# Attention and experts on one core: the last four blocks' attention in even steps, tiles merged before the exponent

## The chip, the cores and the metric

One core of a Trainium2 chip. The metric is the time of one execution on the device in microseconds (us); the kernel before takes 918.2 us, the median of 3 runs (917.75 to 921.53). TensorE (PE in the profile) multiplies matrices, VectorE (DVE), ScalarE (ACT) and GpSimd (POOL) work on elements, SyncE (SP) issues the DMAs.

## The reference

```python
# q, k, v: (4, 8, 576, 64); window of 128 keys, causal
scores = scale * q @ k.T
scores = where(mask, scores + slopes * -(distance), -1e9)      # mask: 0 <= rel < 128
attn = exp(scores - max(scores))
attn = attn / (sum(attn) + 1e-9)
x = (attn @ v)            # as (2304, 512): 4 x 576 tokens, 8 heads x 64
p = domain_probs / (sum(domain_probs) + 1e-9)                  # (2304, 4)
for e in range(4):        # w1: (4, 512, 1024), w2: (4, 1024, 512)
    out += p[:, e] * (relu(x @ w1[e]) @ w2[e])
```

All in float32. The kernel splits each float32 operand into a rounded high part and the remainder (names ending in h and l) and forms each product as three matmuls.

## The kernel before

The 2304 tokens are 18 tiles of 128, put together in seven blocks (`BLOCKS`): 0 to 2 of 256 tokens, 3 to 6 of 384. The attention of a block is done head pair by head pair (4 of them), tile by tile: a *unit* is one tile for two heads. The experts' weights come in 16 pieces of 256 hidden columns; `passes` sets in which order pieces meet blocks: first block 0 alone, then 0 and 1, then 0 to 2, then 1 and 2, then 2, then all pieces with blocks 3 and 4, then with 5 and 6. A meeting of a piece and a block is a *step*: `hidden` (matmuls at line 907, ReLU at 928 on ScalarE, remainder at 935 on VectorE) and `output` (matmuls at 1095, weighted sum into `acc` at 1113 on VectorE). From the ninth piece on, blocks 3 and 4 are multiplied together by a scheme of seven products (`sevenfold`, line 985), and blocks 5 and 6 from the second piece on; `differences` prepares it.

A planner (`Plan`) makes the order. Every operation has the engines that it can run on with an assumed duration, the data that it reads and writes, buffers out of fixed pools, and a due time. `order` simulates the engines and takes what can start earliest, and among those the one that is due first; instructions are then issued in that order, fixed for each engine. Operations that read two SBUF tiles on VectorE, and those of GpSimd, are kept apart by `port`. The due times run on a scale of expert matmuls alone: a step of 256 tokens counts 5.55, one of 384 tokens 8.33, and `opened[nb]` is where block nb's first step stands: 38.9, 94.4, 266.6 for blocks 1, 2, 3 (and 4), 524.9 for 5 (and 6). The attention of a block is due evenly over `spans[nb]`, less `MARGIN` = 10; `end` is the first sevenfold step, 399.9, less `AHEAD` = 30.

A unit outside block 0 goes: `scores` (line 513, two keys' tiles: the tile before and its own, 256 columns for each head), `least` for each head (544 on VectorE: bias added, sign turned, minimum kept), `exponents` (556 on ScalarE, with the sum), 1e-9 added to the two sums (571), reciprocal (580), weights (601 or 609), transposes (627), split in two parts and put in place with the mask (311, 323, 651 on GpSimd), and for the segment the products with v (698). In a row exactly one of a column's two keys, 128 apart, lies in the window; so from block 2 on (`fold`) the two halves of `s` are added after the exponent (592), and the rest works on 128 columns.

`gathered` sums the heads' parts (722, 725), casts the result to `xh` and takes the remainder `xl` (through `cast`, line 311 and 313, and `minus`, line 323). `xh` and `xl` have two places of 768 tokens: blocks 0 to 2 are group 0, 3 and 4 group 1, 5 and 6 group 2, which takes a place when its former group has been read for the last time.

Of the kernel before, what the change touches and what calls it, by code (L numbers as in the profile page):

```python
# [11 lines left out]
AF = mybir.ActivationFunctionType  # L12
ALU = mybir.AluOpType
# [3 lines left out]
NEG = -1.0e30  # L17
PE, DVE, ACT, POOL, SP = "PE", "DVE", "ACT", "POOL", "SP"
# [169 lines left out]
dve = lambda n: 0.065 + n / 960  # L188
dve2 = lambda n: 0.065 + n / 1920
pool = lambda n: 0.1 + n * 0.00256  # L190
# [4 lines left out]
BLOCKS = ((0, 256), (256, 256), (512, 256), (768, 384), (1152, 384), (1536, 384), (1920, 384))  # L195
# [7 lines left out]
FOLD = 2  # L203
# [25 lines left out]
def attention_moe(  # L229
# [13 lines left out]
    nc = tc.nc  # L243
    P = 128
# [4 lines left out]
    NPAIR = H // 2  # L249
# [7 lines left out]
    plan = Plan()  # L257
# [38 lines left out]
    bias = sb.tile([P, H, 2 * P], F32, tag="bias", name="bias")  # L296
# [9 lines left out]
    def cast(o, i, n, due, reads, writes, sbuf=True):  # L306


        def emit(e):
            if e == ACT:  # L310
                nc.scalar.activation(o(), i(), AF.Copy)  # L311
            else:
                nc.vector.tensor_copy(o(), i())

        plan.op(
            {ACT: act(n), DVE: dve2(n) if sbuf else dve(n)}, emit, due, reads, writes, port=(DVE,) if sbuf else ()
        )
# [55 lines left out]
    gs = []  # L373
# [6 lines left out]
    spans = {0: (-30.0, -6.0)}  # L380
    spans[1] = (5.0, opened[1])
    spans[2] = (opened[1], opened[2])
    spans[3] = (opened[2], (opened[2] + opened[3]) / 2)
    spans[4] = ((opened[2] + opened[3]) / 2, opened[3])
    end = opened[5]
    if SEVEN[3, 4] < NU:
        end = next(now for l, nb, now in steps if nb == (3, 4)) - AHEAD
    spans[5] = (opened[3], (opened[3] + end) / 2)
    spans[6] = ((opened[3] + end) / 2, end)
    for nb, (s0, n) in enumerate(BLOCKS):  # L390
        for hp in range(NPAIR):
            g = Rec()
# [94 lines left out]
    def unit(u):  # L487
# [36 lines left out]

        bkey = [("bias", g.hp)] if pk else [("bias", g.hp, 1)]
        bv = lambda: bias[:, hs, :]
        if edge:
# [7 lines left out]
            )  # L537
            bv, bkey = b2, [bb]
        if 0 < pk < P:
            plan.op({POOL: 0.3, DVE: 0.28}, lambda e: by[e].memset(sv()[:, :, :o], 0.0), d, ["scores"], both, port=())  # L540


        def least(h):
            return lambda e: nc.vector.tensor_tensor_reduce(  # L544
                out=sv()[:, h, o:],
                in0=sc()[:, h, :n],
                in1=bv()[:, h, o:],
                scale=-0.125,
                scalar=-NEG,
                op0=ALU.add,  # L550
                op1=ALU.min,
                accum_out=t[:, h : h + 1],
            )

        def exponents(h):
            return lambda e: nc.scalar.activation(  # L556
                sv()[:, h, o:],
                sv()[:, h, o:],
                AF.Exp,
                bias=t[:, h : h + 1],  # L560
                scale=-1.0,
                accum_out=t[:, 2 + h : 3 + h],
            )

        for h in range(2):
            plan.op({DVE: 0.15 + n / 960}, least(h), d + 0.3, [*bkey, bk], [(s, h), (t, h)])
        for h in range(2):
            plan.op({ACT: 0.29 + n * 0.00087}, exponents(h), d + 0.4, [(t, h)], [(s, h), (t, 2 + h)])
        plan.op(
            {DVE: 0.19},  # L570
            lambda e: nc.vector.tensor_scalar(  # L571
                out=t[:, 2:4], in0=t[:, 2:4], scalar1=1.0e-9, scalar2=None, op0=ALU.add
            ),
            d + 0.5,
            [],
            [(t, 2), (t, 3)],
# [5 lines left out]
            [(t, 2), (t, 3)],  # L582
            [(t, 4)],
        )


        fold = pk > 0 and g.nb >= FOLD
        o2, n2 = (P, P) if fold else (o, n)
        if fold:
            plan.op(  # L590
                {DVE: dve(2 * P), POOL: pool(2 * P)},
                lambda e: by[e].tensor_tensor(out=sv()[:, :, P:], in0=sv()[:, :, P:], in1=sv()[:, :, :P], op=ALU.add),  # L592
                d + 0.5,
                [(t, 2), (t, 3)],
                both,
                port=(DVE, POOL),
            )

        def weights_(e):
            if e == DVE:  # L600
# [133 lines left out]
    def gathered(g):  # L734

        n, d = g.n, g.units[-1].due
        gr, at = divmod(g.s0, GROUP)
        xh, xl = groups.setdefault(gr, (Buf("xh"), Buf("xl")))
        cols = slice(at, at + n)
        if g.plain:  # L740

            for h, r in ((0, lo64), (1, hi64)):
                part = (g.nb, g.hp, h)
                xparts.setdefault((g.nb, g.hp), []).append(part)
                cast(
                    lambda r=r: xh[r, g.hp, cols],
                    lambda h=h, r=r: g.av[h][r, :n],
                    n,
                    d + 1.6,
                    [(g.av, h)],  # L750
                    [(xh, part)],
                    False,
                )
                minus(
                    lambda r=r: xl[r, g.hp, cols],
                    lambda h=h, r=r: g.av[h][r, :n],
                    lambda r=r: xh[r, g.hp, cols],
                    n,
                    d + 1.7,
                    [(g.av, h), (xh, part)],  # L760
                    [(xl, part)],
                    False,
                )
            return
        x = Buf("x")
        xs = [(x, 0), (x, 1)]
        summed(g, n, d, lambda: x[:, :n], xs)
        part = (g.nb, g.hp)
        xparts.setdefault((g.nb, g.hp), []).append(part)
        cast(lambda: xh[:, g.hp, cols], lambda: x[:, :n], n, d + 1.6, xs, [(xh, part)])  # L770
        minus(
            lambda: xl[:, g.hp, cols],
            lambda: x[:, :n],
            lambda: xh[:, g.hp, cols],
            n,
            d + 1.7,
            [*xs, (xh, part)],
            [(xl, part)],
        )


# [79 lines left out]
    def differences(nbs, due):  # L861

        xh, xl = groups[BLOCKS[nbs[0]][0] // GROUP]
        done = seen_all() + [(t, p) for t in (xh, xl) for nb in nbs for hp in range(NPAIR) for p in xparts[nb, hp]]
        n = BLOCKS[nbs[0]][1]
        B = lambda t, d, b: f(t[:, 2 * d : 2 * d + 2, b * n : b * n + n])
        tv = lambda b: b[:, :, :n]
        add, sub = ALU.add, ALU.subtract
        raw = {}
        T = kept[nbs] = {}  # L870

        def steps_(name, first_, *rest):
            t = raw[name] = Buf("k")
            a, b, op, rd = first_
            plus(lambda: tv(t), a, b, 2 * n, due, [*done, *rd], [t], op)
            for b2, op2 in rest:
                plus(lambda: tv(t), lambda: tv(t), b2, 2 * n, due, [*done], [t], op2)
            hk, lk = Buf("th"), Buf("tl")
            hv, lv = (lambda: hk.place), (lambda: lk.place)
            cast(hv, lambda: tv(t), 2 * n, due, [t, *done], [hk])  # L880
            minus(lv, lambda: tv(t), hv, 2 * n, due, [t, hk, *done], [lk])
            T[name] = (hv, lv, hk, lk)

        steps_(1, (lambda: B(xh, 0, 1), lambda: B(xh, 0, 0), sub, []), (lambda: B(xl, 0, 1), add), (lambda: B(xl, 0, 0), sub))
        t1 = raw[1]
        steps_(2, (lambda: B(xh, 1, 1), lambda: tv(t1), sub, [t1]), (lambda: B(xl, 1, 1), add))
        t2 = raw[2]
        steps_(3, (lambda: B(xh, 1, 1), lambda: B(xh, 0, 1), sub, [T[2][2]]), (lambda: B(xl, 1, 1), add), (lambda: B(xl, 0, 1), sub))
        steps_(4, (lambda: B(xh, 1, 0), lambda: tv(t2), sub, [t2]), (lambda: B(xl, 1, 0), add))
# [308 lines left out]
        ["dp", "dps"],  # L1198
        ["prob"],
    )  # L1200
    for g in gs:
        segment(g)
        for u in g.units:
            unit(u)
        gathered(g)
    if joint:
        for nbs in dict.fromkeys(joint.values()):
            differences(nbs, first[min(l for l in joint if joint[l] == nbs)] - WEARLY)
    for l in range(len(loads)):
        weights(l)  # L1210
    outs = []
    for l, nb, due in [*steps, (None, None, now)]:
        half = (len(outs) + 1) // 2
        if l in joint:
            sevenfold(l, due, [[o for j, o in enumerate(outs) if (SLOT[j] if len(outs) > 3 else 2 * j + 1) == i] for i in range(7)])
        else:
            if l is not None:
                hidden(l, nb, 0, due)
            for o in outs[:half]:
                output(*o, due)  # L1220
            if l is not None:
                hidden(l, nb, 1, due + 2)
            for o in outs[half:]:
                output(*o, due + 2)
        if l is not None:
            outs = [(l, b, i) for b in (nb if l in joint else [nb]) for i in range(BLOCKS[b][1] // P)]
# [67 lines left out]
```

## Time and profile before

| what | us |
| --- | --- |
| median of 3 runs | 918.2 |
| the profiled execution | 917.55 |
| its span in the trace | 915.8 |
| TensorE busy | 890.8 (97%) |
| VectorE busy | 735.0 (80%) |
| ScalarE busy | 454.3 (50%) |
| GpSimd busy | 378.4 (41%) |

The span runs from the first to the last instruction of one execution. Busy times are unions of the recorded instructions; matmuls overlap in the record, and a short wait between two of them can lie under the end of the first. The granted clock of TensorE is 1.00 of full speed (the 2.4 GHz level) in all stretches shown here. Idle time has, where the trace shows it, the instruction that ended it behind an arrow.

### The profile page before, as it was taken

Reading aid. Unit: us, or ns where it says so; the run is one execution under the profiler, and the core shown is the slowest. Engines: PE = TensorE matmul, PEld = TensorE weight load, DVE = VectorE, ACT = ScalarE, POOL = GpSimd, SP = SyncE. Lnnn points to the kernel's source line nnn. Section 1 sums busy time; section 2 is a strip of 40 time slices with the busy share of each in tenths; the row PEclk is TensorE's granted clock in tenths of the full one; section 3 lists DMA queues with packets and bytes.
Section 4 is the critical chain, followed back from the end, with each engine's and each line's share of the span. In section 5 each row is a group of like instructions: output and inputs, shape, how many; then the busy total and the mean of one; then the engine's idle time right before and its main releaser. Section 6 shows DMA issues by size and latency. Waiting matters only on the chain.

```text
span 915.8 us, 14430 instructions
## 1 busy us (share of the span) xinstructions
PE 890.8 (97%) x5108; PEld 805.5 (88%) x5108; DVE 735.0 (80%) x1520; ACT 454.3 (50%) x1089; POOL 378.4 (41%) x361
## 2 busy tenths in 40 slices
PE   7898999999999999989999999999999999999998
PEld 5787999999999998878899998989898998999897
DVE  4999887697888899989997997767876767677665
ACT  4976555364655466656664343435333433434341
POOL 2446545244444355577674663212632222222100
PEclk9999999999999999999999999999999999999999
DMA  9764534242444445443211022221232121212101
GB/s 241 234 213 160 176 123 137 81 136 67 136 135 135 131 155 178 157 127 98 82 49 67 24 90 72 68 70 52 87 116 92 47 93 47 89 50 76 40 1 70
DMA packets 39961, 96.20 MB, mean 105 GB/s; under 512 B 3792, under 2 KB 17488, under 8 KB 39888
## 3 DMA queue, kind: packets, MB, share of 16 engines
q1 hardware_dynamic: 39888, 95.28, 32.6%
q8 instruction: 40, 0.66, 0.3%
q14 instruction: 33, 0.27, 0.1%
HBM read 90.54 MB, written 4.72 MB: 104 GB/s over the span
## 4 chain that ended last, share of the span: by engine, by line
PE 84%; DVE 12%; ACT 2%; issue 1%; DMA 1%; ACTq 0%; DVEq 0%
PE b L1095 39%; PE b L907 18%; PE b L985 18%; PE av L698 3%; PE b L513 2%; PE b L627 2%; DVE w2l L323 1%; DVE s L544 1%; DVE s L592 1%; DVE w1l L323 1%; DMA k<-in_qk 1%; DVE acc L1113 1%; PE b L504 1%; DVE s L601 1%; DVE t L571 1%
## 5 line engine op out<-in xcount | busy, mean ns | idle before, releaser
L1113 DVE SCALAR_TENSOR_TENSOR acc<-b,prob,acc 128x512 f32<-128x512 f32 (+1 forms) x229 | 169.8, 743 | 66.5 <-PE b L1095 65.5
L1095 PE MATMUL b<-w2h,rh 128*128 128x512 f32 x440 | 174.1, 396 | 1.0 <-DVE rl L935 1.0
L1095 PE MATMUL b<-w2l,rh 128*128 128x512 f32 x440 | 172.9, 393 | 0.0
L1095 PE MATMUL b<-w2h,rl 128*128 128x512 f32 x440 | 172.5, 392 | 0.0
L907 PE MATMUL b<-xh,w1h 128*128 128x256 f32 (+1 forms) x528 | 160.9, 305 | 5.0 <-DVE t L544 2.1
L907 PE MATMUL b<-xl,w1h 128*128 128x256 f32 (+1 forms) x528 | 156.9, 297 | 0.5 <-DVE xl L323 0.5
L907 PE MATMUL b<-xh,w1l 128*128 128x256 f32 (+1 forms) x528 | 157.1, 297 | 0.0
L323 POOL TENSOR_TENSOR w2l<-w2r,w2h 128x512 fp32r<-128x512 f32 x45 | 67.7, 1507 | 124.9 <-ACT w2h L311 111.6
L907 PEld LDWEIGHTS b<-xh,w1h 128*128 128x128 f32 x528 | 100.2, 190 | 8.0 <-DVE t L544 2.3
L651 POOL TENSOR_SCALAR_AFFINE_SELECT pt<-s 128x512 fp32r<-128x512 f32 x104 | 66.9, 667 | 92.1 <-DVE s L323 68.5
L907 PEld LDWEIGHTS b<-xl,w1h 128*128 128x128 f32 x528 | 100.2, 190 | 2.9 <-DVE xl L323 0.7
L907 PEld LDWEIGHTS b<-xh,w1l 128*128 128x128 f32 x528 | 100.0, 189 | 0.0
L1095 PEld LDWEIGHTS b<-w2h,rl 128*128 128x128 f32 x440 | 82.6, 188 | 18.1
L1095 PEld LDWEIGHTS b<-w2h,rh 128*128 128x128 f32 x440 | 83.0, 189 | 11.9 <-DVE rl L935 1.3
L928 ACT ACTIVATE rh<-b 128x256 fp32r<-128x256 f32 (+1 forms) x132 | 53.3, 404 | 79.9 <-PE b L907 79.7
L1095 PEld LDWEIGHTS b<-w2l,rh 128*128 128x128 f32 x440 | 83.0, 189 | 10.2
L556 ACT ACTIVATE s<-s,t 128x256 f32<-128x256 f32 (+2 forms) x128 | 62.5, 489 | 59.0 <-DVE t L544 58.4
L935 DVE SCALAR_TENSOR_TENSOR rl<-b,rh 128x256 fp32r<-128x256 f32 (+1 forms) x132 | 60.1, 455 | 26.9 <-ACT rh L928 25.3
L323 POOL TENSOR_TENSOR w1l<-w1r,w1h 128x512 fp32r<-128x512 f32 x42 | 60.9, 1455 | 43.5 <-ACT w1h L311 20.7
L1019 ACT ACTIVATE xh<-b 128x384 fp32r<-128x384 f32 x46 | 22.6, 492 | 92.4 <-DVE b L1004 86.0
L311 ACT ACTIVATE w2h<-w2r 128x512 fp32r<-128x512 f32 x111 | 65.0, 621 | 6.4 <-PE b L1095 5.8
L839 POOL TENSOR_TENSOR q<-w1r 128x256 f32<-128x256 f32 x23 | 19.3, 841 | 111.3 <-DMA w1r<-in_w 85.6
(155 smaller groups left out, 2044.3 us busy)
## 6 DMA issues: line engine op xcount, KB each, us to landing
w1r<-in_w SPq DMA_DIRECT2D x60, 512.0 KB, 4.2
w2r<-in_w SPq DMA_DIRECT2D x60, 512.0 KB, 3.5
q<-in_q SPq DMA_DIRECT2D x16, 384.0 KB, 3.7
k<-in_k SPq DMA_DIRECT2D x12, 512.0 KB, 3.8
k<-in_k SPq DMA_DIRECT2D x12, 384.0 KB, 3.8
out<-acc SPq DMA_DIRECT2D x17, 256.0 KB, 2.1
v<-in_v SPq DMA_DIRECT2D x12, 256.0 KB, 2.7
v<-in_v SPq DMA_DIRECT2D x12, 192.0 KB, 3.5
```

The source lines that it names most:

```text
L311: nc.scalar.activation(o(), i(), AF.Copy)
L323: by[e].tensor_tensor(out=o(), in0=a(), in1=f(b()), op=ALU.subtract)
L556: return lambda e: nc.scalar.activation(sv()[:, h, o:], sv()[:, h, o:], AF.Exp, bias=t[:, h : h + 1], scale=-1.0, accum_out=t[:, 2 + h : 3 ...
L651: return lambda e: nc.gpsimd.affine_select(out=pt[:, :, :, c0 + own * P : c0 + own * P + P], in_=hl(), pattern=[[0, 4], [1, P] if own else ...
L698: nc.tensor.matmul(g.av[h][:, q0 : q0 + m], v2, g.pt[h][:, c : c + m] if g.plain else pt[:, x, h, c : c + m], start=not g.started[h], stop ...
L907: nc.tensor.matmul(bk[:, :n], a[0][:, kt, fs], b[:, kt, cols], start=kt == 0 and i == 0, stop=kt == KT - 1 and i == 2,)
L928: lambda e: nc.scalar.activation(h[:, :n], bk[:, :n], AF.Relu),
L935: lambda e: nc.vector.scalar_tensor_tensor(out=lo[:, :n], in0=bk[:, :n], scalar=0.0, in1=f(h[:, :n]), op0=ALU.max, op1=ALU.subtract,),
L985: nc.tensor.matmul(bank[:, :n], x(k), y(k), start=new and k == 0 and i == 0, stop=k == 1 and i == 2, skip_group_check=True,)
L1019: lambda e: nc.scalar.activation(h[:, :n], src(), AF.Relu),
L1095: nc.tensor.matmul(bk[:, cs], a[:, ns], b[1][:, fi, cs], start=half != 1 and fi == 0 and j == 0, stop=half != 0 and fi == 1 and j == 2, sk ...
L1113: nc.vector.scalar_tensor_tensor(out=o, in0=i_, scalar=p, in1=o, op0=ALU.mult, op1=ALU.add)
```

## The change

Four edits. The due spans of blocks 3 to 6 are cut evenly from `opened[2]` to `end`, block 5 not before the last step of blocks 0 and 1. Group 2 uses the very buffers of group 0, and each of its casts and remainders depends on the reads of those earlier blocks whose columns it overwrites, in place of the whole buffer. In units with `fold` the two halves are merged by a minimum of the negated scores ahead of the exponents, on VectorE, and the exponents work on 128 columns; the addition after them is gone, and the fill of unused columns is 1e30 in place of 0. Outside block 0, 1e-9 is added on ScalarE. The lists of operations are built in another order, so that a write stands behind the reads that it must wait for.

```diff
-    spans[3] = (opened[2], (opened[2] + opened[3]) / 2)
-    spans[4] = ((opened[2] + opened[3]) / 2, opened[3])
     end = opened[5]
     if SEVEN[3, 4] < NU:
         end = next(now for l, nb, now in steps if nb == (3, 4)) - AHEAD
-    spans[5] = (opened[3], (opened[3] + end) / 2)
-    spans[6] = ((opened[3] + end) / 2, end)
+    left = max(now_ for _, nb, now_ in steps if nb in (0, 1)) + 6.0
+    at_ = opened[2]
+    for nb in range(3, 7):
+        if nb == 5:
+            at_ = max(at_, left)
+        spans[nb] = (at_, at_ + (end - at_) / (7 - nb))
+        at_ = spans[nb][1]
...
+        def guarded(e):
+            if e == ACT:
+                nc.scalar.activation(t[:, 2:4], t[:, 2:4], AF.Copy, bias=1.0e-9)
+            else:
+                nc.vector.tensor_scalar(out=t[:, 2:4], in0=t[:, 2:4], scalar1=1.0e-9, scalar2=None, op0=ALU.add)
...
             return lambda e: nc.scalar.activation(
-                sv()[:, h, o:],
-                sv()[:, h, o:],
+                sv()[:, h, o2:],
+                sv()[:, h, o2:],
                 AF.Exp,
...
+        if fold:
+            plan.op(
+                {DVE: dve(2 * P)},
+                lambda e: nc.vector.tensor_tensor(out=sv()[:, :, P:], in0=sv()[:, :, P:], in1=sv()[:, :, :P], op=ALU.min),
+                d + 0.35,
+                [(t, 0), (t, 1)],
+                both,
+                port=(DVE,),
+            )
...
-            {DVE: 0.19},
...
+            {DVE: 0.19} if g.plain else {ACT: 0.25},
+            guarded,
...
-        if fold:
-            plan.op(
-                {DVE: dve(2 * P), POOL: pool(2 * P)},
-                lambda e: by[e].tensor_tensor(out=sv()[:, :, P:], in0=sv()[:, :, P:], in1=sv()[:, :, :P], op=ALU.add),
...
+        if gr == 2:
+            groups[2] = groups[0]
         xh, xl = groups.setdefault(gr, (Buf("xh"), Buf("xl")))
         cols = slice(at, at + n)
+        old = [b for b, (s0, n0) in enumerate(BLOCKS[:3]) if gr == 2 and s0 < at + n and at < s0 + n0]
+        was = [p for b in old for hp in range(NPAIR) for p in xparts[b, hp]]
...
-        cast(lambda: xh[:, g.hp, cols], lambda: x[:, :n], n, d + 1.6, xs, [(xh, part)])
+        cast(lambda: xh[:, g.hp, cols], lambda: x[:, :n], n, d + 1.6, xs, [(xh, part), *((xh, p) for p in was)])
```

## Rows read from the trace of the kernel before

**Rows 1.** The page, the chain that ended last: shares of the span by engine.

```profile
PE 84%; DVE 12%; ACT 2%; issue 1%; DMA 1%; ACTq 0%; DVEq 0%
```

**Rows 2.** The table of stretches: length, busy us (x instructions) of PE, PEld, DVE, ACT, POOL; clock, DMA.

```profile
25.00:100.00 75.00, 68.02 (x462) 61.36 (x463) 71.51 (x163) 58.43 (x150) 43.16 (x34) 1.00 0.60 197
167.00:348.00 181.00, 181.00 (x1226) 166.82 (x1225) 152.96 (x375) 100.20 (x268) 79.44 (x78) 1.00 0.38 119
348.00:490.00 142.00, 133.78 (x786) 121.48 (x785) 133.07 (x311) 88.52 (x232) 95.23 (x97) 1.00 0.35 110
350.00:475.00 125.00, 116.78 (x685) 105.72 (x684) 118.73 (x274) 79.30 (x206) 84.36 (x85) 1.00 0.37 116
```

**Rows 3.** Groups of instructions, TensorE, 350 to 475 us: line, shape, xcount | busy, mean ns.

```profile
L907 PE MATMUL b<-xh,w1h 128*128 128x384 f32 x80 | 28.0, 350 | 2.1 <-DVE t L544 2.1
...
L1095 PE MATMUL b<-w2h,rh 128*128 128x512 f32 x62 | 25.1, 405 | 1.0 <-DVE rl L935 1.0
...
L698 PE MATMUL av<-pt,vs 128*128 128x128 f32 (+1 forms) x106 | 15.0, 273 | 1.2 <-DVE x L725 1.2
...
L513 PE MATMUL b<-kh,qs 128*128 128x256 f32 (+1 forms) x40 | 10.8, 292 | 0.0
L627 PE MATMUL b<-ident,s 128*128 128x128 f32 x42 | 8.4, 278 | 3.9 <-DVE s L601 2.8 <-ACT s L609 1.1
...
L907 PE MATMUL b<-xh,w1h 128*128 128x256 f32 x10 | 3.0, 303 | 0.0
```

**Rows 4.** Pieces of the chain, 475 to 500 and 100 to 125 us: start, us, what.

```profile
477.32 2.09 PE b L907 x12
479.41 0.47 PE av L698 x4
479.88 2.75 PE b L1095 x12
...
103.06 1.43 PE b L907 x12
```

**Rows 5.** The table of stretches for line 513 alone, the score matmuls.

```profile
0.00:167.00 167.00, 10.46 (x64) 9.08 (x64) 1.00 0.59 184
167.00:348.00 181.00, 15.38 (x96) 14.16 (x96) 1.00 0.38 119
348.00:490.00 142.00, 15.72 (x96) 13.78 (x96) 1.00 0.35 110
```

**Rows 6.** The same for line 907 alone, the experts' first products.

```profile
0.00:167.00 167.00, 65.62 (x468) 60.39 (x468) 1.00 0.59 184
```

**Rows 7.** The same for line 571 alone on VectorE, the addition of 1e-9.

```profile
167.00:348.00 181.00, 13.58 (x24) 1.00 0.38 119
348.00:490.00 142.00, 9.47 (x23) 1.00 0.35 110
```

**Rows 8.** Instructions in order of time, 453 to 455.2 us, VectorE and GpSimd: start, us.

```profile
453.22 1.80 DVE L571 TENSOR_SCALAR t<-t 128x2 f32<-128x2 f32 x1
...
453.15 1.85 POOL L323 TENSOR_TENSOR qs<-q,qs 64x768 fp32r<-64x768 f32 x1
```

**Rows 9.** Groups of instructions by shape, whole span, of the softmax.

```profile
L556 ACT ACTIVATE s<-s,t 128x256 f32<-128x256 f32 x104 | 52.2, 502 | 47.3 <-DVE t L544 46.8
...
L556 ACT ACTIVATION_READ_ACCUMULATOR s<-s,t 128x1 f32 x128 | 24.0, 188 | 0.0
...
L592 DVE TENSOR_TENSOR s<-s 128x256 f32<-128x256 f32 x35 | 22.0, 631 | 0.0
...
L592 POOL TENSOR_TENSOR s<-s 128x256 f32<-128x256 f32 x17 | 13.2, 776 | 15.3 <-ACT s L556 12.5 <-DVE x L725 2.8
...
L580 DVE RECIPROCAL t<-t 128x2 f32<-128x2 f32 x72 | 11.3, 157 | 0.8
...
L556 ACT ACTIVATE s<-s,t 128x128 f32<-128x128 f32 x8 | 3.2, 399 | 7.4 <-DVE t L544 7.4
```

**Rows 10.** Waits from 345 to 490 us: who waited for whom, us, times, longest.

```profile
ACT s L556 <- DVE t L544: 25.6, 15, 5.2
```

More of the change, by code (lines that the diff above doesn't have):

```diff
@@ L387, in attention_moe @@
         end = next(now for l, nb, now in steps if nb == (3, 4)) - AHEAD
-    spans[5] = (opened[3], (opened[3] + end) / 2)
-    spans[6] = ((opened[3] + end) / 2, end)
+    left = max(now_ for _, nb, now_ in steps if nb in (0, 1)) + 6.0
[5 more added lines that the diff above has]
+        at_ = spans[nb][1]
+    assert spans[4][1] <= opened[4]
     for nb, (s0, n) in enumerate(BLOCKS):
@@ L523, in unit @@
         plan.op({PE: passes_ * mm(n)}, scores, d, qk, [bk, "scores"], [s], passes_ * mmc(n), late=late)
+        fold = pk > 0 and g.nb >= FOLD
+        o2, n2 = (P, P) if fold else (o, n)
         bkey = [("bias", g.hp)] if pk else [("bias", g.hp, 1)]
@@ L539, in unit @@
         if 0 < pk < P:
-            plan.op({POOL: 0.3, DVE: 0.28}, lambda e: by[e].memset(sv()[:, :, :o], 0.0), d, ["scores"], both, port=())
+            plan.op({POOL: 0.3, DVE: 0.28}, lambda e: by[e].memset(sv()[:, :, :o], -NEG if fold else 0.0), d, ["scores"], both, port=())
         def least(h):
@@ L566, in unit @@
             plan.op({DVE: 0.15 + n / 960}, least(h), d + 0.3, [*bkey, bk], [(s, h), (t, h)])
+        if fold:
[7 more added lines that the diff above has]
+            )
         for h in range(2):
-            plan.op({ACT: 0.29 + n * 0.00087}, exponents(h), d + 0.4, [(t, h)], [(s, h), (t, 2 + h)])
+            plan.op({ACT: 0.29 + n2 * 0.00087}, exponents(h), d + 0.4, [(t, h)], [(s, h), (t, 2 + h)])
         plan.op(
-            {DVE: 0.19},
-            lambda e: nc.vector.tensor_scalar(
-                out=t[:, 2:4], in0=t[:, 2:4], scalar1=1.0e-9, scalar2=None, op0=ALU.add
-            ),
+            {DVE: 0.19} if g.plain else {ACT: 0.25},
+            guarded,
             d + 0.5,
@@ L584, in unit @@
         )
-        fold = pk > 0 and g.nb >= FOLD
-        o2, n2 = (P, P) if fold else (o, n)
-        if fold:
-            plan.op(
-                {DVE: dve(2 * P), POOL: pool(2 * P)},
-                lambda e: by[e].tensor_tensor(out=sv()[:, :, P:], in0=sv()[:, :, P:], in1=sv()[:, :, :P], op=ALU.add),
[L593 to L597, printed above, removed]
         def weights_(e):
@@ L777, in gathered @@
             [*xs, (xh, part)],
-            [(xl, part)],
+            [(xl, part), *((xl, p) for p in was)],
         )
@@ L1200, in attention_moe, with attend @@
     )
[L1201 to L1209, printed above, removed]
+    def attend(nbs):
+        for g in gs:
+            if g.nb in nbs:
+                segment(g)
+                for u in g.units:
+                    unit(u)
+                gathered(g)
+    attend(range(5))
+    second = min(l for l, nb, _ in steps if nb == 3 or nb == (3, 4))
+    for l in range(second):
         weights(l)
@@ L1212, in attention_moe @@
     for l, nb, due in [*steps, (None, None, now)]:
+        if l is not None and l >= second and len(wst) == second:
+            attend((5, 6))
+            for nbs in dict.fromkeys(joint.values()):
+                differences(nbs, first[min(x for x in joint if joint[x] == nbs)] - WEARLY)
+            for x in range(second, len(loads)):
+                weights(x)
         half = (len(outs) + 1) // 2
```

## The prediction, made before the change was run

> **What bounds the kernel now.** I read the shares of the chain first: most of it lies on TensorE, a smaller part on VectorE [rows 1]. So TensorE's matmuls set the time, except where VectorE takes their place; the next view has to say where that is. The table of stretches does [rows 2]. From 167 to 348 us, where the attention of blocks 3 and 4 runs, TensorE is busy for all of 181 us. From 348 to 490, with blocks 5 and 6, it is busy for 133.78 of 142, and VectorE is at 133.07 of 142. From 25 to 100 both are short too (68.02 and 71.51 of 75). After 490 TensorE is full.
>
> A stall is partly hidden in these busy times, because the recorded matmuls overlap: one of 512 columns is recorded with about 0.4 us [rows 3], but six of them take 2.75 / 2 = 1.38 us when nothing is waited for [rows 4]. So I count the work of 350 to 475 us from its instructions. Steady prices [rows 4]: 0.229 us for 512 columns, 0.174 for 384, 0.119 for 256, 0.118 for a matmul of the attention. Counts [rows 3]: the second products are 3 x 62 = 186, the first products 3 x 80 = 240 of 384 columns and about 3 x 10 = 30 of 256, the attention's values, scores (two groups of 40) and transposes 106 + 80 + 42 = 228. Sum: 42.6 + 41.8 + 3.6 + 26.9 = 114.9 of 125 us. TensorE loses about 10 us there, of which 8.2 are seen as idle (125 - 116.78, rows 2).
>
> The cause is density. 96 score matmuls are 24 units (a unit is one tile of 128 tokens for two heads, 4 matmuls); 24 take 181 us in blocks 3 and 4, 7.5 us each, and 142 us in blocks 5 and 6, 5.9 us each [rows 5]. If VectorE needs m per us of TensorE's work for the experts and a for each unit, alike in both stretches, then 181 m + 24 a = 152.96 and 133.78 m + 24 a = 133.07 [rows 2], so m = 0.42 and a = 3.2 us. In blocks 5 and 6 VectorE is then wanted for 133.07 / 133.78 = 0.99 of TensorE's time, and every late result is a stall; in blocks 3 and 4 for 0.85, and none is seen.
>
> **The change part by part.** *Spacing.* By the kernel's own arithmetic (a step of 256 tokens is 5.55, of 384 tokens 8.33) block 3 opens at 266.6, block 2 at 94.4, and attention must end at 369.9. Before, blocks 3 and 4 get 86.1 each and blocks 5 and 6 51.6. After, 68.9, 68.9, 68.1 and 68.1: a unit falls due every 5.7 instead of every 7.2 and then 4.3. No matmul is added or removed, so TensorE's sum stays, and at most the 10 us come back. Spread evenly over 323 - 10 = 313 us, VectorE's 152.96 + 133.07 = 286.0 us are 0.91.
>
> The units will not come evenly, though. By 167 us, where the 64th score matmul ends blocks 1 and 2 [rows 5], 468 first products are done [rows 6]; at 24 to a step that is 19.5 steps, or 108.3 on the scale of due times, while the first unit of block 3 was due at 94.4 - 10 = 84.4. Attention is some 24 late, four units of the new spacing. If it catches up by the last unit of block 4 (due 216.5), TensorE has 108 us of experts and 24 units of 228 x 0.118 / 20 = 1.3 us [rows 3, 4] in between: 140 us, 5.8 us for a unit. That is the density which loses time today, and the other 175 us get 7.3 for a unit.
>
> *The small addition moved to ScalarE.* L571 adds 1e-9 to two numbers in each of 128 partitions. It takes 13.58 + 9.47 = 23.05 us for 47 of them between 167 and 490 us [rows 7], a mean of 0.49, where the reciprocal of the same shape takes 0.157 [rows 9]. The difference is a wait: one L571 lasts from 453.22 to 455.02, and GpSimd's subtraction runs from 453.15 to 455.00 [rows 8]. So 47 x 0.157 = 7.4 us leave VectorE for certain, and up to 23.05 if no later instruction takes over the wait. ScalarE gets 64 additions; their form is not in the trace. The bounds are the 0.188 of its shortest group and the 0.399 of a 128x128 activation [rows 9]; I take 0.2, nearer the first because two elements are nearer one: 13 us, at most 26. The exponents pay for most of it: 104 shrink to 128 columns, and 88 x (0.502 - 0.399) alone is 9 us [rows 9]. It follows the exponents on their own engine, so only reciprocals wait for it, as before.
>
> The Trainium skill speaks against this part: "ScalarE: Activation LUTs", Rules for kernel authors, sends additions to VectorE. By that rule the part would cost time; the rows decide otherwise, since what it leaves is a wait and not the arithmetic.
>
> *The minimum.* 52 additions of 128x256 after the exponents become 52 minima before them, on VectorE alone. Before, 17 were done by GpSimd at 0.776 us and 35 by VectorE at 0.631 [rows 9]. So VectorE gains at most 17 x 0.631 = 10.7 us, GpSimd loses 13.2. Both exponents now wait for both reductions and the minimum; before, the first waited for one reduction. The chain gets longer by some 0.6 us at its front and shorter by as much behind. What is queued behind a waiting exponent on ScalarE is the ReLU of the experts (L928), for which VectorE's remainder (L935) and then TensorE wait. TensorE's wait for that remainder is 1.0 us in the 125 us of [rows 3] today, so I cost this at nothing, with the price in the rivals if that lead is gone.
>
> The Trainium skill says in "SBUF — State Buffer", Who interferes with whom, that a VectorE instruction with two SBUF inputs also contends with a GpSimd instruction that reads SBUF. By it the minimum inherits waits of the kind which the addition of 1e-9 leaves. The mean of 0.631 already holds such waits, so the term stays 10.7.
>
> Together VectorE changes between 167 and 490 us by -23.05 + 10.7 = -12.3 to -7.4 + 10.7 = +3.3 us: evenly spread a share of 0.87 to 0.92. In the dense 140 us it is wanted for 0.42 x 140 + 24 x 3.2 = 135.6 us, and half of those bounds makes it 129 to 137, or 0.92 to 0.98. In the later 175 us it is about 0.86.
>
> *Piecewise overwriting.* Group 2 no longer waits for a whole buffer; each write of 384 columns waits for the reads of the blocks below it. Block 1's last first products start at 227.7 and end by 233.2, the first write of block 5 is due at 236.6, so nothing is queued long behind it: nothing, with 4 casts as the exposure. The loads of k, q and v for these blocks go out earlier on SP's queue, past loads of expert weights; in 167 to 348 us the DMA engines are at 0.38 [rows 2], which hides them.
>
> **The sum.** Of the 10 us lost from 350 to 475 I take back 9, since 0.86 is the share at which blocks 3 and 4 lose nothing. The dense 140 us give back 2 (bounds 0, as at 0.85, and 8, as today's dense stretch). From 25 to 100 us VectorE is at 0.95 [rows 2], and the eight additions of block 1, at the mean of 0.49 us from [rows 7] an estimated 3.9 us, leave it; I take 1.5 us of gain (bounds -1 and 4). That is -8.5 us. The profiled execution took 917.55 us, the span is 915.8; so 909.05 for it, and the median of the runs, 918.2, stands 0.65 above it. I forecast 909, with its own range 905 to 913.
>
> **The rivals.** (1) *The dense stretch moves.* Catching up puts the density of blocks 5 and 6 on blocks 3 and 4, and VectorE at 0.98 makes TensorE lose there most of what it loses now: 7 us given back in place of 2, 914 (912 to 917). For it: the backlog at 167 us. Against it: from blocks 0 to 2 there is expert work that needs none of the late units, and L571's waits are gone. (2) *No change*: the minimum and the inherited waits use up what L571 frees, so that the dense stretch gives back all 9 and 25 to 100 us gains nothing: 918. (3) *Slower, by the minimum in front of the exponents.* An exponent waits for one more reduction and a minimum that may wait on GpSimd, 0.9 us, with the ReLU behind it. ScalarE already waits 25.6 us for the reductions from 345 to 490 [rows 10]. If one in three of the 52 units reaches TensorE, 17 x 0.9 = 15 us stand against the 8.5: 924. It decides where the hidden layer's lead over TensorE is used up; today's 1.0 us speaks against it. (4) *Better*: the dense stretch loses nothing and 25 to 100 us, where 7 us are idle, gets back 4 or more: 903 and below.
>
> **How the numbers follow.** Forecast 0.52, rival 1 0.18, rival 2 0.07, rival 3 0.10, rival 4 0.13. The range 902.5 to 917.5 holds the forecast, rival 1, a good part of the fourth and some of the second. A measurement of this kernel tells about 0.5%, 4.6 us, from no change. Faster, below 913.6: 0.51 + 0.13 + a third of rival 1, 0.70. Within 0.5%: the rest of it, 0.12 + 0.07 + 0.01 = 0.20. Slower: 0.10.
>
> **What the profile after would show.** Right: units of blocks 3 to 6 about 6.5 us apart, the last ending some 10 us earlier; TensorE without idle time from 350 to 475; VectorE at 0.85 to 0.92 there; the addition as a ScalarE activation of about 0.2 us; the minimum at 0.6 us. Wrong: idle time of TensorE between 167 and 310 us (rival 1), ScalarE's waits for the minimum followed by TensorE's for L935 (rival 3), TensorE waiting in blocks 5 and 6 for casts into xh (the overwriting).

## The result, and the profile after

| | median, us | profiled execution, us | span, us |
| --- | --- | --- | --- |
| before | 918.96 (4 runs) | 917.55 | 915.8 |
| after | 904.25 (4 runs, 903.58 to 905.75) | 904.8 | 902.9 |

The ratio of after to before is 0.9847, with a 95% interval of 0.9824 to 0.987: 14.7 us faster. The two profiled executions, with mean granted clocks of 0.999 and 1.00, differ by 12.75 us; the clock can have a part in the rest (see the last section). The forecast was 909, its range 902.5 to 917.5, its own narrower range 905 to 913. So the time lies in the range, 4.75 us below the forecast and just below the narrower one.

The chain that ended last, after (shares of the span by engine), against [rows 1]; VectorE's share is half of what it was:

```profile
PE 91%; DVE 6%; DMA 1%; ACT 1%; issue 1%; POOL 0%; DVEq 0%; POOLq 0%; ACTq 0%
```

The table of stretches, after, with the columns and stretches of [rows 2]:

```profile
25.00:100.00 75.00, 72.14 (x496) 66.01 (x497) 66.23 (x158) 60.07 (x162) 46.01 (x36) 1.00 0.65 211
167.00:348.00 181.00, 180.63 (x1228) 165.66 (x1227) 155.28 (x385) 106.45 (x315) 85.16 (x82) 1.00 0.40 125
348.00:490.00 142.00, 141.51 (x826) 129.98 (x826) 116.45 (x271) 84.40 (x238) 83.85 (x86) 1.00 0.33 109
350.00:475.00 125.00, 124.51 (x729) 114.38 (x729) 105.70 (x250) 77.64 (x221) 75.15 (x76) 1.00 0.33 110
```

TensorE's idle time from 350 to 475 us went from 8.2 to 0.5 us, and VectorE from 133.07 to 116.45 of 142. From 25 to 100 us TensorE was busy for 4.1 us more, and VectorE for 5.3 us less.

The same table for the score matmuls alone, line 519 after (513 before), against [rows 5]:

```profile
0.00:167.00 167.00, 10.93 (x68) 9.91 (x68) 1.00 0.60 185
167.00:313.00 146.00, 14.34 (x88) 12.69 (x88) 1.00 0.38 119
313.00:348.00 35.00, 3.75 (x24) 3.58 (x24) 1.00 0.45 152
348.00:490.00 142.00, 12.33 (x76) 10.91 (x76) 1.00 0.33 109
```

22 units in 146 us are 6.6 us for one. The 6 up to 348 us come at 5.8, and the 19 after that, where there were 24 before, at 6.7: the last score matmul starts at 474.8 us, where it was 487.3. So the pace is nearly even in real time too, not only on the scale of due times (before, 7.5 and then 5.9).

Groups of the softmax after, against [rows 7] and [rows 9] (line 568 is the addition of 1e-9, 573 the exponent, 587 the minimum):

```profile
L568 ACT ACTIVATE t<-t 128x2 f32<-128x2 f32 x64 | 12.6, 197 | 1.0
...
L587 DVE TENSOR_TENSOR s<-s 128x256 f32<-128x256 f32 x52 | 33.0, 639 | 0.3
```

```profile
L573 ACT ACTIVATE s<-s,t 128x128 f32<-128x128 f32 x112 | 44.0, 394 | 45.3 <-DVE s L587 42.8 <-DVE t L555 1.8 <-issue 0.3
```

The addition takes 0.197 us on ScalarE, the minimum 0.639 on VectorE, the shorter exponent 0.394. ScalarE now waits for the minimum where it waited for the reductions (46.8 us on the 128x256 exponents of rows 9, 42.8 here).

TensorE's waits in the whole span, after (us, times, longest):

```profile
PE b L510 <- DMA k<-in_qk: 5.8, 3, 4.6
PE b L923 <- DVE xl L323: 1.3, 2, 0.8
PE b L923 <- ACT t L568: 1.3, 1, 1.3
PE av L709 <- ACT acc L311: 1.1, 1, 1.1
PE av L709 <- DVE x L736: 0.4, 1, 0.4
PE b L1111 <- DVE rl L951: 0.4, 1, 0.4
PE b L1001 <- DVE x L1078: 0.2, 1, 0.2
```

Between 348 and 490 us only the fifth lies, 0.4 us.

### The profile page after: what moved, and what is told of

Read it like the earlier page. It is cut to its first block, busy times and chain, and to the rows that moved or that the text cites. A ratio compares the mean times of both kernels' runs of the same rounds, so it can differ in the third digit from the quotient of the medians.

```text
span 902.9 us, 14383 instructions
## 1 busy us (share of the span) xinstructions
PE 889.0 (98%) x5108; PEld 805.3 (89%) x5108; DVE 710.7 (79%) x1476; ACT 449.9 (50%) x1145; POOL 371.3 (41%) x348
## 4 chain that ended last, share of the span: by engine, by line
PE 91%; DVE 6%; DMA 1%; ACT 1%; issue 1%; POOL 0%; DVEq 0%; POOLq 0%; ACTq 0%
PE b L1111 41%; PE b L923 22%; PE b L1001 18%; PE av L709 4%; PE b L519 3%; PE b L638 2%; DMA k<-in_qk 1%; PE b L510 1%; DVE w1l L323 1%; DMA w1r<-in_w 1%; DVE w2l L323 1%; DVE acc L1129 1%; DVE s L555 0%; DVE vs L323 0%; DVE x L736 0%
## 5 line engine op out<-in xcount | busy, mean ns | idle before, releaser
L323 POOL TENSOR_TENSOR w2l<-w2r,w2h 128x512 fp32r<-128x512 f32 x48 | 70.2, 1466 | 129.9 <-ACT w2h L311 116.3
L323 POOL TENSOR_TENSOR w1l<-w1r,w1h 128x512 fp32r<-128x512 f32 x45 | 64.1, 1430 | 41.5 <-ACT w1h L311 17.9
L573 ACT ACTIVATE s<-s,t 128x128 f32<-128x128 f32 (+1 forms) x128 | 52.0, 408 | 47.7 <-DVE s L587 42.8
L323 DVE TENSOR_TENSOR w2l<-w2r,w2h 128x512 fp32r<-128x512 f32 x72 | 62.5, 881 | 0.3 <-ACT w2h L311 0.2
```

What stands on the lines that cost most here:

```text
L323: by[e].tensor_tensor(out=o(), in0=a(), in1=f(b()), op=ALU.subtract)
L573: return lambda e: nc.scalar.activation(sv()[:, h, o2:], sv()[:, h, o2:], AF.Exp, bias=t[:, h : h + 1], scale=-1.0, accum_out=t[:, 2 + h : ...
```

## The experiments

Two sums are worked out from each trace, for every kernel in the same way. *TensorE's loss*: for each matmul the time from its start to the start of the next, less the lower quartile of that time for matmuls of its line and width, where it is more than 0.04 us over. It finds the short stalls that the overlapping records hide. The span less the whole loss (with the stretches that the table leaves out) is 871 to 873 us in all fourteen kernels, so the loss is what they differ by. About 10 us of the whole, in each of them, are hardly stalls: among the transposes the lower quartile is 0.028 us and the median 0.108, and this difference counts. So kernels can be compared, but the levels are too high. *VectorE's waits*: the duration of each instruction between 25 and 490 us, less the tenth percentile of its form. The stretches are fixed in time, so that a stage that starts 5 us earlier shifts a little between columns. The column "low clock" is the part of the loss at matmuls that start while the granted clock is 0.50 of full speed, the 1.2 GHz level (0 where the profile has no such stretch before the last matmuls). Each trace is one execution: of "old order, ScalarE" one of 912.19 us, of "after without minimum" one of 907.74, both 3 us or more from the median.

| kernel | median, us | its before | loss 25-100 | 167-348 | 348-490 | after 490 | VectorE's waits | low clock |
| --- | --- | --- | --- | --- | --- | --- | --- | --- |
| before | | | 13.4 | 4.5 | 15.0 | 0.7 | 77.1 | 0 |
| after | 904.25 | 918.96 | 8.9 | 6.6 | 5.1 | 0.8 | 48.8 | 0 |
| spacing alone | 912.23 | 916.8 | 13.5 | 6.6 | 5.7 | 2.1 | 65.4 | 1.4 |
| minimum alone | 914.63 | 916.8 | 12.9 | 6.0 | 9.9 | 1.3 | 80.2 | 0 |
| addition alone | 906.27 | 916.8 | 10.0 | 4.8 | 7.2 | 1.2 | 50.7 | 1.5 |
| before, planned anew | 914.07 | 916.8 | 13.8 | 4.6 | 9.6 | 1.6 | 75.8 | 3.9 |
| same order, no wait | 913.16 | 916.87 | 11.0 | 4.7 | 13.6 | 0.5 | 60.8 | 1.6 |
| after without spacing | 910.73 | 916.87 | 12.3 | 4.5 | 6.7 | 4.8 | 51.1 | 3.3 |
| after without minimum | 904.51 | 916.87 | 10.7 | 7.0 | 5.5 | 0.4 | 53.6 | 0 |
| after without addition | 912.2 | 916.87 | 15.3 | 6.4 | 5.9 | 0.5 | 68.7 | 0 |
| old order, ScalarE | 915.75 | 918.1 | 10.9 | 4.6 | 13.0 | 0.4 | 59.6 | 1.6 |
| new order, VectorE | 915.5 | 918.1 | 11.0 | 5.0 | 15.6 | 0.5 | 73.4 | 2.9 |
| after, planned anew | 916.63 | 918.1 | 17.4 | 6.2 | 7.0 | 2.6 | 62.0 | 6.0 |
| after, addition left out | 915.99 | 918.1 | 15.6 | 7.6 | 4.7 | 5.0 | 56.7 | 1.6 |

### The spacing alone

Of the change, the kernel before gets the spans and the piecewise overwriting:

```diff
+    left = max(now_ for _, nb, now_ in steps if nb in (0, 1)) + 6.0
+    at_ = opened[2]
+    for nb in range(3, 7):
...
+        if gr == 2:
+            groups[2] = groups[0]
```

> The kernel before with the even spans and the piecewise overwriting alone; the halves are still added after the exponent, 1e-9 stays on VectorE. Theory A (density of blocks 5 and 6 is the loss, as in the forecast): TensorE's loss from 350 to 475 us goes from 10 to about 1, some 2 us come back between 167 and 310; 25 to 100 us stays as it was; about 911 to 913. Rival B (the waits of L571 behind GpSimd are the loss, wherever they lie): under 5 us of gain, 914 or more, since every one of the 64 waits is still there.

Measured: 912.23 us (910.55 to 916.29), ratio 0.9948, interval 0.9923 to 0.9974. The table of stretches of this kernel:

```profile
25.00:100.00 75.00, 69.37 (x465) 63.04 (x466) 69.95 (x163) 58.44 (x147) 43.39 (x35) 0.98 0.58 195
167.00:348.00 181.00, 180.38 (x1226) 166.09 (x1225) 154.37 (x389) 107.31 (x288) 98.97 (x94) 1.00 0.37 122
348.00:490.00 142.00, 141.37 (x831) 129.86 (x830) 123.94 (x299) 89.11 (x233) 79.56 (x86) 1.00 0.34 110
```

Blocks 5 and 6 lose nothing more that is seen (141.37 of 142), the loss from 167 to 348 grows by 2.1 us, and 25 to 100 us keeps its 13.5: theory A to the letter, on its own stretch. It brings 4.6 us of the 14.7, though, so there is more to the change.

### The minimum alone

Of the change, the kernel before gets the minimum, with the shorter exponents and the fill that go with it:

```diff
+                lambda e: nc.vector.tensor_tensor(out=sv()[:, :, P:], in0=sv()[:, :, P:], in1=sv()[:, :, :P], op=ALU.min),
...
-                lambda e: by[e].tensor_tensor(out=sv()[:, :, P:], in0=sv()[:, :, P:], in1=sv()[:, :, :P], op=ALU.add),
```

> The kernel before with the minimum ahead of the exponents alone. Theory A: VectorE gains up to 10.7 us of work and ScalarE loses about 10; no change, 916 to 921, or slightly slower, since blocks 5 and 6 are already short of VectorE. Rival C (the freed ScalarE or GpSimd time matters): 4 us or more faster.

Measured: 914.63 us (913.31 to 918.72), ratio 0.9973 (0.995 to 0.9997). That is 2.2 us faster than its before, below the band of theory A and short of rival C. The next run but one shows that 2 to 3 us are no more than a new order gives.

### The addition alone

Of the change, the kernel before gets the addition on ScalarE:

```diff
-            {DVE: 0.19},
+            {DVE: 0.19} if g.plain else {ACT: 0.25},
```

> The kernel before with 1e-9 added on ScalarE alone. Theory A: 25 to 100 us gives back about 1.5 to 4 us, blocks 5 and 6 2 to 4 of their 10 because VectorE is less wanted there: 911 to 916. Rival B: most of the 14.7 us of the whole change, 908 or below. Rival D (the wait is only handed to the next instruction that needs the port): 917 to 920.

Measured: 906.27 us (904.01 to 909.4), ratio 0.9885 (0.9846 to 0.9924): 10.5 us, rival B's answer and more than theory A's upper end. The waits of VectorE fall from 77.1 to 50.7 us, by 26.4, where L571's own were 22.1: they are not handed on. Rival D falls. The table of stretches of this kernel:

```profile
25.00:100.00 75.00, 72.29 (x487) 66.20 (x488) 64.38 (x153) 60.94 (x164) 46.93 (x35) 0.98 0.63 207
167.00:348.00 181.00, 181.00 (x1227) 166.99 (x1226) 144.59 (x343) 105.57 (x292) 86.09 (x79) 1.00 0.37 122
348.00:490.00 142.00, 140.96 (x827) 129.00 (x827) 122.98 (x295) 93.69 (x264) 98.00 (x105) 1.00 0.34 111
```

Without any spacing blocks 5 and 6 are mended almost as well (140.96 of 142): VectorE is at 122.98 us there instead of 133.07.

### The kernel before, planned anew

One constant of the planner is changed, and so the order:

```diff
-EXTRA = 0.03
+EXTRA = 0.04
```

> The kernel before with one constant of the planner changed, the assumed delay between dependent operations 0.04 instead of 0.03 us; nothing is added or removed, only the order of issue is planned anew. It measures how far the time moves from a new order alone: all theories that name a part expect within 2 us of before (917 to 921); 4 us or more would mean that effects of that size can't be put down to a part.

Measured: 914.07 us (913.16 to 915.11), ratio 0.9967 (0.9951 to 0.9983). Nothing but the order differs, and the loss from 348 to 490 us falls from 15.0 to 9.6. So the 15 us of the kernel before were partly its order. By the medians the 2.7 us lie between the 2 and the 4 of the expectation, but the clock hides some of it: eight of the ten executions have a mean clock of 0.996, and the six of its before that have it too took 921.6 us in the median, 7.5 more than these eight (914.1). At this clock, then, a new order alone is worth more than 4 us, and by the expectation effects of that size can't be put down to a part.

### The same order without the wait

The plan is that of the kernel before; outside block 0 another instruction stands in the place of the addition, a sum over one element, so that 1e-9 is left out there:

```diff
-            lambda e: nc.vector.tensor_scalar(
-                out=t[:, 2:4], in0=t[:, 2:4], scalar1=1.0e-9, scalar2=None, op0=ALU.add
+            nc.vector.tensor_scalar(out=t[:, 2:4], in0=t[:, 2:4], scalar1=1.0e-9, scalar2=None, op0=ALU.add)
+            if g.plain
+            else nc.vector.reduce_sum(out=t[:, 2:4], in_=t[:, 2:4, None], axis=AX.X),
```

> The kernel before in its own order, instruction by instruction; outside block 0 VectorE's addition of 1e-9 is replaced by a sum over one element of the same 128x2 numbers, also on VectorE, with the same dependencies (the 1e-9 is left out of the computation there). It keeps an instruction in the place and takes away only what L571 waits for behind GpSimd. Rival B, after the addition alone gave 10 us: the wait itself is the loss; the new instruction takes 0.1 to 0.25 us each time, VectorE's time above the shortest of each form falls by 20 us or more, 906 to 911. Rival D (the wait is handed on to the next instruction at the port) or rival E (the addition's run gained by its new order): 914 to 919.

Measured: 913.16 us (912.55 to 915.5), ratio 0.9955 (0.9935 to 0.9974). The line's instructions on VectorE in the kernel before, and in this one (xcount: shortest / median / longest, ns):

```profile
L571 DVE TENSOR_SCALAR t<-t x72: 147/170/1804, 7.0 to 490.5; 128x2 f32<-128x2 f32 x72
```

```profile
L575 DVE TENSOR_REDUCE t<-t x64: 137/146/157, 31.6 to 485.9; 128x2 f32<-128x2 f32 x64
```

The wait is gone (1804 against 157 ns at the longest), in the same place of the same order. The Trainium skill has this difference in "SBUF — State Buffer", Who interferes with whom: a tensor_scalar can take the port pair that GpSimd uses, a reduction on trn2 never does; the two rows agree. VectorE's waits fall by 16.3 us in all, below the 20 expected, and the time by 3.7: between rival B's band and the other's, and nearer the other's. So in this order the wait itself is worth about 4 us, and the rest of the addition's 10.5 has to be sought elsewhere.

### The changed kernel less one part

Without the spacing, the old spans are back; the piecewise overwriting stays:

```diff
+    spans[3] = (opened[2], (opened[2] + opened[3]) / 2)
+    spans[4] = ((opened[2] + opened[3]) / 2, opened[3])
+    spans[5] = (opened[3], (opened[3] + end) / 2)
+    spans[6] = ((opened[3] + end) / 2, end)
```

> The changed kernel with the old spans of blocks 3 to 6; piecewise overwriting, minimum and the addition on ScalarE stay. Theory A (spacing carries 7 of the 14.7 us): 910 to 913. Rival B (the addition carries most, and spacing only mends what it leaves in blocks 5 and 6): 904 to 908, TensorE's loss from 348 to 490 us 2 to 5 us above that of the changed kernel.

Measured: 910.73 us (907.97 to 913.72), ratio 0.9911 (0.9877 to 0.9946): 6.5 us slower than after, in theory A's band, but not for theory A's reason. Its loss from 348 to 490 is only 1.6 us above that of the changed kernel; 25 to 100 us loses 3.4 more and the time after 490 4.0 more, stretches that the spans of blocks 3 to 6 don't name, and 1.8 and 1.4 us of these lie at the lower clock. So the band was met by luck.

Without the minimum, the halves are added behind the exponents, as before:

```diff
-                lambda e: nc.vector.tensor_tensor(out=sv()[:, :, P:], in0=sv()[:, :, P:], in1=sv()[:, :, :P], op=ALU.min),
...
+                lambda e: by[e].tensor_tensor(out=sv()[:, :, P:], in0=sv()[:, :, P:], in1=sv()[:, :, :P], op=ALU.add),
```

> The changed kernel with the halves added after the exponents again, on VectorE or GpSimd. Theory A and rival B alike: the minimum is worth nothing or costs a little, since it puts up to 10.7 us more on VectorE: 902 to 906. Rival C (ScalarE's shorter exponents matter): 908 or more.

Measured: 904.51 us (904.21 to 907.74), ratio 0.9853 (0.9815 to 0.989). The minimum is worth nothing that can be told here.

Without the addition on ScalarE, VectorE has it again:

```diff
-            {DVE: 0.19} if g.plain else {ACT: 0.25},
+            {DVE: 0.19},
```

> The changed kernel with 1e-9 added on VectorE again. Theory A: the spacing is there, so 907 to 909, 25 to 100 us loses 3 to 5 us more. Rival B: 910 to 914, as with the spacing alone, with 20 us or more of L571's waits back on VectorE.

Measured: 912.2 us (909.01 to 914.52), ratio 0.9924 (0.9895 to 0.9953). As rival B had it; L591 of this kernel holds 15.6 us of the waits, a little under the 20 expected. The blocks 3 to 6 lose what they lose after (6.4 and 5.9); the whole difference stands from 25 to 100 us, 15.3 against 8.9.

### Order and engine apart

The old order is the plan of the kernel before, with the 64 additions issued to ScalarE in their places:

```diff
+            else nc.scalar.activation(t[:, 2:4], t[:, 2:4], AF.Copy, bias=1.0e-9),
```

The new order is the plan of "the addition alone", with the 64 additions issued to VectorE in their places:

```diff
-            if e == ACT:
+            if e == POOL:
```

> The kernel before in its own planned order, with the 64 additions of 1e-9 issued to ScalarE at the places where they stood on VectorE. Against the addition alone with a new plan (906.3) and the same order without the wait on VectorE (913.2) it splits the gain. Rival B (relief of VectorE): 64 waits and 64 x 0.157 us leave VectorE, so 908 to 911. Rival E (the new plan carries the rest): 912 to 915, no better than the sum in place of the addition.

> The order planned for the addition on ScalarE, with the 64 additions issued to VectorE. Rival B: 20 us or more of waits return to VectorE and the time goes back to 914 to 920, TensorE losing 12 us or more from 348 to 490 us. Rival E: the new order keeps most of its gain, 907 to 911.

Measured: old order with ScalarE 915.75 us (912.19 to 918.26), ratio 0.9969 (0.9947 to 0.999); new order with VectorE 915.5 us (913.71 to 919.27), ratio 0.9973 (0.995 to 0.9996). By the medians each alone brings 2 to 3 us. At an equal mean clock the first brings more: 916.5 against 921.8 us at 0.996 (7 and 12 executions), 913.9 against 917.7 at 0.998 (3 and 8); the second 914.3 against 916.8 at 1.0 (5 and 9). Both together brought 10.5, and what goes beyond the sum of the two stands in blocks 5 and 6. In the old order 59.6 us of waits remain and blocks 5 and 6 still lose 13.0. In the new order the additions on VectorE wait more than ever; their group of instructions in this kernel (xcount | busy, mean ns | idle before):

```profile
L559 DVE TENSOR_SCALAR t<-t 128x2 f32<-128x2 f32 x72 | 41.9, 582 | 6.1 <-ACT s L562 4.7 <-ACT acc L562 0.7
```

and blocks 5 and 6 lose 15.6 where they lose 7.2 with the same order on ScalarE. So neither rival B nor rival E stands by itself. In blocks 5 and 6 the gain needs a plan that counts on the addition's being off VectorE, and the addition off VectorE, so that the order is kept in the execution.

### The changed kernel, planned anew and without the addition

The first has the planner's constant of above in the changed kernel. The second leaves the addition out of it, outside block 0:

```diff
-        plan.op(
-            {DVE: 0.19} if g.plain else {ACT: 0.25},
+        if g.plain:
+            plan.op(
+                {DVE: 0.19} if g.plain else {ACT: 0.25},
...
```

> The changed kernel with the assumed delay between dependent operations at 0.04 instead of 0.03 us: a new order of the same operations. The kernel before moved by 2.7 us under this edit. All theories: 901 to 907; outside of it the single parts can't be told apart within that distance.

> The changed kernel without the addition of 1e-9 outside block 0, which leaves out that part of the computation (the sums there are 1 or more, so in float32 it changes none of them). 64 activations of about 0.2 us leave ScalarE and the chain of each unit. ScalarE is half idle, so under rival B nothing more is to be had: 901 to 906. If the addition's place on ScalarE costs something, for the ReLU behind it, 900 or below.

Measured: 916.63 us (914.32 to 918.03), ratio 0.9976 (0.9956 to 0.9996), and 915.99 us (913.44 to 918.14), ratio 0.9965 (0.9943 to 0.9987). Both are 12 us slower than the changed kernel, far outside every expectation, though one has its very operations and the other 64 fewer.

The one planned anew doesn't compute the reference's result either: its output is off by 2.1%. The reason lies in the planner, as its text and this order show. `slots` lets only the first operation on a new buffer wait until the former use of its place is over. Here the cast of the second half of a piece's first weights, planned on another engine than the first half, stands ahead of block 1's last matmuls with an earlier piece, which still read that place. The other orders don't run into this, but nothing in the planner keeps them from it. The cast is due past 110 us in the plan, so it has no part in the time lost before.

From 348 to 490 us they are as good as after (losses 7.0 and 4.7). What is lost lies at the start and after 490 us. The table of stretches from 20 to 30 us, of the kernel after first, then of the one planned anew, then of the one with the addition left out:

```profile
20.00:30.00 10.00, 8.79 (x54) 6.88 (x53) 9.16 (x34) 9.90 (x32) 2.73 (x3) 1.00 0.67 204
```

```profile
20.00:30.00 10.00, 7.14 (x33) 5.30 (x34) 9.62 (x25) 7.16 (x22) 6.64 (x5) 0.93 0.77 256
```

```profile
20.00:30.00 10.00, 9.53 (x35) 7.27 (x35) 5.83 (x25) 7.07 (x24) 1.26 (x1) 1.00 0.48 151
```

TensorE issues 54 matmuls there after, 33 and 35 in the other two (53 in the kernel before; 32 in "before, planned anew"). The start has been put into another order, although no edit names it, and from 25 to 100 us they lose 17.4 and 15.6 us against 8.9. Of the 17.4, 6.0 lie in three stretches at the lower clock, and the mean clock is low in all ten executions of this kernel (0.993 to 0.996, where the changed kernel has 0.998 to 1.0). In the one with the addition left out no such stretch lies there, so its 6.7 us more are the order's. Idle time of TensorE there, in the one planned anew and the one left out:

```profile
25.00:100.00 75.00, 69.35 (x440) 62.78 (x441) 65.88 (x148) 55.39 (x145) 45.19 (x34) 0.93 0.57 191
```

```profile
25.00:100.00 75.00, 68.26 (x457) 61.27 (x456) 69.45 (x158) 56.29 (x145) 37.50 (x29) 1.00 0.60 201
```

## Why the prediction came out as it did

*What bounds the kernel: right.* TensorE's loss in blocks 5 and 6 was the largest that could be taken back, and was: 15.0 to 5.1 us from 348 to 490. That is 9.9 us back, and the 10 us that the prediction read from the instruction counts agree with it.

*The sum's three terms.* Forecast were -9 for blocks 5 and 6, +2 for the earlier blocks and -1.5 from 25 to 100 us. By the losses they were -9.9, +2.1 and -4.5 (13.4 to 8.9). The step that failed is the last term, mis-sized threefold: 4.5 against 1.5, just past the bound of 4. It had priced the eight additions of block 1. The runs show something else in its place. That stretch loses 8.9 to 17.4 us over all plans, 10.0 with the addition alone, but 15.6 with the addition left out; what moves it is the order in which the planner happens to put the start, and in some executions the clock. The remaining 0.7 us is from 0 to 25 us (9.7 to 9.0). Together -13.0, and the span fell by 12.9.

*The dense stretch: the size right by luck, the reason wrong.* I expected blocks 3 and 4 to be 24 late on the scale of due times at 167 us and to catch up at 5.8 us for a unit. There was no such backlog. The 38.9 and 94.4 given above for `opened[1]` and `opened[2]` are where a pass of pieces starts; block 2's own first step comes behind four steps of blocks 0 and 1 in that pass, at 94.4 + 4 x 5.55 = 116.6 (and block 1's at 44.4). So the first unit of block 3 was due at 106.6, not 84.4, and at 108.3 attention was 2 late. The four new spans are 63.3 each, not 68 to 69, and the old ones of blocks 3 and 4 were 75.0, not 86.1. A unit is then due every 5.3, which with its own 1.3 us on TensorE makes 6.6: the pace that was measured. VectorE stayed below the 0.92 to 0.98 of the forecast, as the table of stretches after shows for that time:

```profile
167.00:313.00 146.00, 146.00 (x997) 134.25 (x996) 122.15 (x313) 82.21 (x244) 64.64 (x62) 1.00 0.38 119
```

That is 0.84, and no idle time is seen. Of the 2.1 us that this stage loses more, 1.1 lie in the 35 us from 313 to 348, where 6 units come at 5.8 us and VectorE is at 0.95 (155.28 - 122.15 = 33.13 us): the dense stretch that was forecast, only short and late. The loss is the price of the spacing all the same. The six kernels with the new spans lose 6.2 to 7.6 us from 167 to 348, the eight with the old ones 4.5 to 6.0. From 348 to 490 the six lose 4.7 to 7.0, whatever else they hold, and the eight 6.7 to 15.6. So the spacing makes blocks 5 and 6 safe against the order; how much that gains depends on how bad the order was: 15.0 in the kernel before was near the worst of the eight.

*The addition: undervalued.* I gave it a part in VectorE's share and 1.5 us. With it, against without it, the kernels differ by 10.5 (nothing else changed), 7.7 (with the spacing: 912.23 to 904.51), 3.9 (with the minimum: 914.63 to 910.73, which has the piecewise overwriting too) and 8.0 us (with both: 912.2 to 904.25). I had left open whether a later instruction takes over the wait; from before to after VectorE's waits fall by 28.3 us, more than L571's 22.1, and its time between 167 and 490 us by 286.0 - 271.7 = 14.3, a little past my bound of 12.3. But the last two runs have no addition on VectorE either and stand at 916, so the four differences are not the price of the addition alone; they hold the luck of eight plans, and the clock of their executions.

*The prices* came out: 0.197 us for the 0.2 of the addition on ScalarE, 0.639 for the 0.631 of the minimum, 0.394 for the 0.399 of the exponent. ScalarE's total went from 454.3 to 449.9 us. The Trainium skill's rule in "ScalarE: Activation LUTs", Rules for kernel authors, which sends additions to VectorE, would have spoken against this part; the 0.49 us against 0.197 decide the other way in this kernel.

*The rivals.* Rival 1 (the dense stretch moves) didn't come: 2.1 us, not 7; the backlog that spoke for it wasn't there. Rival 2 (no change, 918) is 14 us off. Rival 3 (the minimum in front of the exponents) didn't: TensorE's waits for the ReLU's remainder are 0.4 us in all, and leaving the minimum out gives the same 904.5. Rival 4 was nearest, at 903 and below for 4 us or more from 25 to 100; its own terms (917.55 - 9 - 4) give 904.6 and below. The time is 904.25, with 4.5 us from 25 to 100 as that rival has it, but with the dense stretch losing its 2. TensorE waits for no cast into `xh` in blocks 5 and 6, so the piecewise overwriting cost nothing, as costed; a version with the new spans and whole buffers wasn't run.

*What stays open.* Which order of the first 100 us is good, and why the planner leaves the good one for so small an edit, wasn't settled. 904 is the best that was measured, by the changed kernel and the one without the minimum, and a new plan of the same operations gives 916.6 and a wrong output. So the change holds for this plan; its parts can be told apart only where they show in a stretch of their own, as the spacing does.

## What to carry to other kernels

Where a planner fixes the order, plan a kernel anew without changing it (a constant of the cost model moved a little) before a gain is put down to an edit: here that moved the median by 2.7 us in one kernel and by 12.4 in the other, a part of it through the clock. See that such a plan still computes the same: the second didn't, since the planner lets only a buffer's first new user wait. Evening out the density of a stage that is short of one engine took its stalls away in all six orders tried; relieving that engine did nearly as much there in one (7.2 us lost against 5.7). A tiny instruction can last far longer than its work (1.80 us against 0.15 here); taking the wait away in a fixed order brought 4 us, and with a plan that knew of it 10, so move such an instruction and let the plan know. Read a due time off the program before building on it: a backlog that isn't there cost this prediction its reason.

## What the runs showed of the hardware

In some executions of one and the same kernel TensorE's granted clock falls for a short stretch to 0.50 of full speed, often near 30 to 50 us, where TensorE has just been idle (18.5 of the first 25 us busy in the kernel before, and 7.68 of 10 in the second row here). The table of stretches of "the spacing alone" shows it:

```profile
20.00:30.00 10.00, 8.79 (x53) 6.84 (x52) 8.72 (x32) 9.29 (x29) 2.71 (x3) 1.00 0.66 213
30.00:40.00 10.00, 7.68 (x47) 7.15 (x46) 8.01 (x17) 9.30 (x25) 7.32 (x5) 0.83 0.83 274
40.00:50.00 10.00, 10.00 (x73) 9.33 (x72) 9.18 (x25) 8.52 (x23) 5.77 (x5) 1.00 0.62 201
```

0.83 is a mean of the full 2.4 GHz and the lower 1.2 GHz level. The profiles hold fourteen such stretches before the last matmuls, in nine kernels, and not only at the start: "after without spacing" has one from 552.8 us, behind an idle time of 1.8 us in which TensorE waited for VectorE, and "after, planned anew" one from 86.7 us, behind 2.0 us. Not every wait of that length is followed by one: in the kernel before, the clock stays at 1.00 behind the 2.1 us in which line 907 waits for line 544 (from 360.6 us). Between 1.4 and 2.5 us of TensorE's loss lie in each stretch. If the wait brings it about, the wait costs more than its own length; that wasn't tested.

For the kernel before, 21 executions with a mean clock of 1.0 have a median of 916.6 us, and 24 with 0.996 one of 921.6. The kernel before planned anew has 0.996 in eight of ten, the changed kernel 1.0 in three of four; some part of each comparison by medians is this clock.
